# Attention and a routed expert layer on one core: the place of "V times the experts' rows" and of the divisions in the queues, and a second key slot of each head that meets V in float32

## The chip, the cores and the metric

The kernel runs on one core of a Trainium2 chip. The metric is device time in microseconds (us) of that core. Each core has TensorE (PE in the profile; its weight loads are PEld), VectorE (DVE), ScalarE (ACT), GpSimd (POOL) and SyncE (SP), which here only issues DMAs. Each engine works through its own queue in the order of the program and waits at an instruction whose operands or buffers aren't ready.

## The reference

Attention with rotary positions over 4 batches of 8 heads, 576 positions, 64 columns a head; its output, as 2304 tokens of 512 columns, goes through a layer of 8 experts of which each token uses the one with the largest logit.

```python
q_rot, k_rot = (rotate(q), rotate(k))
scores = scale * np.matmul(q_rot, k_rot.transpose(0, 1, 3, 2))
attn = np.exp(scores - np.max(scores, axis=-1, keepdims=True))
attn = attn / (np.sum(attn, axis=-1, keepdims=True) + 1e-09)
x = np.matmul(attn, v)             # then (tokens, heads * 64)
logits = (x / norm(x)) @ (emb / norm(emb)).T / tau
expert_idx = np.argmax(logits, axis=1)
out[mask] = gate_w[mask, None] * (np.maximum(x[mask] @ w1[e], 0.0) @ w2[e])
```

## The kernel before

**Attention.** The 32 heads are 16 pairs (`i`), four to a batch. In a pair the 576 keys of each head are cut into slots of 128; the two last halves of 64 share slot 4, so a pair has 9 slots `s`: 0 to 3 and half of 4 for the first head, 5 to 8 and the other half for the second. For each slot:

- `smm` (tile `st`, lines L208 and L211): TensorE makes the scores, keys in the partitions, 576 queries in the columns.
- `sexp` (tile `p`, L221): ScalarE takes exp into a float32 tile. Its upper 16 bits of each number are read as bfloat16 (`hi`).
- `ssub` (L230): VectorE writes `p - hi` as float16 into the lower half (`lo`). A slot that is `whole` (key slot 0 of each head before) has no `ssub`.
- `maxmm`/`maxmm2` and `maxred` (tile `mx`, L171, L183 and L187): the scores of a later pair, queries in the partitions, and VectorE's maximum over them; `mx` 4 and pairs `s`, `s+5`.
- `pv` (tile `pv`, L246 to L251): probabilities times V for 128 queries, over the five key slots of the head. A slot that isn't whole costs three 16-bit matmuls (`hi` with V's upper part, `hi` with its lower part, `lo` with its upper part); a whole slot costs one float32 matmul, which the trace shows as two.

`st` and `mx` share three PSUM buffers; a new tile takes the buffer whose reader stands earliest in the program, and TensorE waits until that reader is done. `pv` of query slots 0 to 4 lies in PSUM bank 0, of 5 to 8 in bank 1.

V's tile has 73 columns a part: one for the row sum, 64 of V and 8 that are V times the experts' rows, made by `ve`: part 0 are five float32 matmuls into bank 1 (tile `ve`, L112, ten in the trace), then ScalarE copies them out (L116 and L117) and VectorE makes their lower part (L118). `pvend` makes the reciprocals of the row sums on VectorE (L262 and L265), and `pvscale` divides on ScalarE: two instructions (L276 and L277) for each query slot, which are what frees the bank.

**The order** is written out by hand: each step is put at a time `g` in units of one slot (`g0 = 9 * i` is the start of a pair's scores, its `pv` follow `PVL` = 7.5 slots later), all are sorted by it and issued so on every engine. `TIMES` holds these numbers. `spare` finds places for the routing steps that need a PSUM bank, from the list `free` (from, to, bank; in slots of the `pv` period). A batch's squares (`square`) and the write of its rows (`write_x`) follow its last pair.

**Routing and experts.** Ranks and lists of tokens are made on VectorE with a few matmuls (`rank`, `list`); 22 tiles of tokens then go through the experts, their float32 weights being split into two float16 parts by ScalarE (L683) and VectorE (L684).

The slots' places in the order before:

```python
y = g0 + PVL - 9 + cfg.get("vet", 1) + (cfg.get("ve0", 0) if i == 0 else 0)
ev("VE0", y, ve, i, 0)
ev("VE1", y + .9, ve, i, 1)
```

Of the kernel before, what the change touches and what calls it, by code (L numbers as in the profile page):

```python
# [16 lines left out]
B, H, S, D = 4, 8, 576, 64  # L17
# [1 line left out]
SHIFT = 44.375  # L19
VS = 16.0  # L20

NF = 1
GUARD = float(1e-9 * np.exp(0.125 * SHIFT) * VS)


# [7 lines left out]
SY = SX * SW * SW  # L33

ORDER = ((0, 0, 0), (1, 0, 0), (0, 0, 1), (1, 0, 1), (0, 1, 0), (1, 1, 0))
TIMES = {"pe1": 1.06, "pvlead": 7.5, "mend": 11.5, "fin": 3, "w": 0.3, "pbufs": 13, "vat": -1, "med": 0.3, "sst": 1.6, "mct": 0.25, "pvt": 0.3, "pe0": 0.9, "d": 0.6, "rdt": 0.9, "e": 0.5, "c0": 135, "fin2": 2.5, "sq": 0.8, "max0": [[-21, 0.5], [-5, 1], [4.5, 0.9]], "start": [-30, -13, -4, 2.6], "le": -3.5, "vet": 1.2, "mmt": 0.2, "mlead": 14, "klo": 1, "me0": [-13.5, 6.6], "mdir": 3, "ve0": -16, "v0": 3, "pl": [[0, 0, 0, 0], [0, 3, 2, 5]], "setup": [-59.5, -25, -20.9, -19.2, -59.4, -14], "l3": -12, "rk": 14, "ls": 52, "dt": 0.6, "t0": 148.5, "ta": 0.25, "wlead": 10, "cut1": 126, "glead": 20, "s": 0.6, "fin3": -0.45, "r01": [[-30.0, -29.1, -28.2, -27.3, -24.6, -26.4, -25.5, -23.7, -22.8, -21.0], [-25, -24.9, -24.8, -15.5, -14, -20.8, -20.7, -20.6, -15, -13.5]], "bw": 0, "cp": [0, 2, 4, 6], "c0d": 1, "lg1": 0.5, "free": [[2.3, 2.3, 1], [3.5, 3.5, 1], [6.2, 6.2, 0]], "fgap": 1.2}


def attention(tc, ctx0, ctx, ctx2, ins, xs, R, at, bank, cfg):
# [34 lines left out]
    st = {}  # L74
# [31 lines left out]
    def ve(i, k):  # L106

        d = V16[i % NV]
        if k == 0:
            ps = st["ve", i] = bank("ve", 1)  # L110
            for j in range(5):
                nc.tensor.matmul(ps[:, 0:80].rearrange("p (h j e) -> p j h e", h=2, j=5)[:, j], lhsT=st[i]["vt"][:, j], rhs=R.enB[:, i % 4],  # L112
                                 start=True, stop=True)
        else:
            ps = st.pop(("ve", i))[:, 0:80].rearrange("p (s e) -> p s e", e=8)
            nc.scalar.activation(out=d[:, :, 65:73], in_=ps, func=AF.Copy, scale=VS)  # L116
            nc.scalar.activation(out=V32[i % NV][:, :, :, 65:73], in_=ps.rearrange("p (h k) e -> p h k e", h=2)[:, :, 0:NF], func=AF.Copy, scale=VS)  # L117
# [163 lines left out]
    PVL = cfg.get("pvlead", 7)  # L281
# [3 lines left out]
    start = cfg["start"]  # L285
    O = cfg.get("o", {})

    def ev(key, g, f, *a):
        at(g + O.get(key, 0), f, *a)

    for i in range(NPAIR):
        g0 = 9 * i
        r0 = start[i] if i < len(start) else g0 - L - RL
        rdt = cfg.get("rdt", .85)
        if i == 1:
            for nm in "qk":
# [455 lines left out]
class Schedule:  # L752
# [3 lines left out]
    def at(self, g, f, *a):  # L756
        self.T.append((g, len(self.T), f, a))
# [13 lines left out]
def build(tc, ins, out, cfg=None):  # L771
    cfg = {**TIMES, **(cfg or {})}
    nc = tc.nc
    with ExitStack() as ctx:
# [10 lines left out]
        R = Routing(tc, ctx, ins, xs, bank)  # L785
        rp = ctx.enter_context(tc.tile_pool(name="raw", bufs=1))
        raw = [rp.tile([128, 1024], F32, name=f"raw{c}") for c in range(8)]
        sc = Schedule()
        mctx, actx2, actx, actx0 = [ctx.enter_context(ExitStack()) for _ in range(4)]
        if True:  # L790
            PVL = attention(tc, actx0, actx, actx2, ins, xs, R, sc.at, bank, cfg)
# [81 lines left out]
            at = lambda G, *a: sc.at(T0 + DT * G, *a)  # L873
# [114 lines left out]
```

## Time and profile before

| | us |
|---|---|
| median of three runs | 629.57 (628.33 to 630.09) |
| the profiled execution's own time | 627.74 |
| its span, first to last instruction | 626.0 |

The profiled execution has 1.7 us around its span and is 1.8 us under the median. Busy times of the whole span are means over stages with different limits: a start of about 60 us, the 16 pairs, a change-over near 350 to 390 us, and the experts' tiles until the end. The pairs have to be read by themselves.

### The profile page before, as it was taken

Reading aid. Unit: us, or ns where it says so; the run is one execution under the profiler, and the core shown is the slowest. Engines: PE = TensorE matmul, PEld = TensorE weight load, DVE = VectorE, ACT = ScalarE, POOL = GpSimd, SP = SyncE. Lnnn points to the kernel's source line nnn. Section 1 sums busy time; section 2 is a strip of 40 time slices with the busy share of each in tenths; the row PEclk is TensorE's granted clock in tenths of the full one; section 3 lists DMA queues with packets and bytes.
Section 4 is the critical chain, followed back from the end, with each engine's and each line's share of the span. In section 5 each row is a group of like instructions: output and inputs, shape, how many; then the busy total and the mean of one; then the engine's idle time right before and its main releaser. Section 6 shows DMA issues by size and latency. Waiting matters only on the chain. (4 is left out here: it accounts for less than half of the span.)

```text
span 626.0 us, 16246 instructions
## 1 busy us (share of the span) xinstructions
PE 536.7 (86%) x6222; PEld 400.3 (64%) x6222; DVE 514.5 (82%) x750; ACT 394.5 (63%) x848; POOL 256.3 (41%) x162
## 2 busy tenths in 40 slices
PE   1689788877987798778788898999999999999993
PEld 0336657665765575656566786777768677776861
DVE  6987987788778977896777556569999999999991
ACT  2152564567546755544745776258989899898972
POOL 6667764467446754471000333221414233242311
PEclk9999997889878988787878899999999999999997
DMA  8486645465645475513401731137888312441100
GB/s 292 117 235 176 161 134 160 120 165 164 166 118 132 136 217 135 148 31 92 141 24 39 268 116 35 37 102 235 282 309 279 134 35 72 168 176 52 52 20 29
DMA packets 42914, 86.13 MB, mean 138 GB/s; under 512 B 8390, under 2 KB 25670, under 8 KB 42832
## 3 DMA queue, kind: packets, MB, share of 16 engines
q1 hardware_dynamic: 39312, 74.46, 39.9%
q0 software_dynamic: 3520, 10.58, 5.3%
q8 instruction: 51, 0.84, 0.6%
q14 instruction: 31, 0.25, 0.1%
HBM read 115.84 MB, written 10.56 MB: 202 GB/s over the span
## 5 line engine op out<-in xcount | busy, mean ns | idle before, releaser
L684 DVE SCALAR_TENSOR_TENSOR w<-raw,w 128x1024 f16<-128x1024 f32 x148 | 177.1, 1237 | 9.3 <-ACT w L683 9.1
L221 ACT ACTIVATE p<-st 128x576 f32<-128x576 f32 x144 | 94.7, 662 | 122.4 <-PE st L211 122.3
L683 ACT ACTIVATE w<-raw 128x1024 f16<-128x1024 f32 x148 | 148.6, 1056 | 0.2
L187 DVE TENSOR_REDUCE m<-mx 128x1 f32<-128x576 f32 x144 | 105.0, 748 | 36.5 <-PE mx L171 19.2
L230 DVE TENSOR_TENSOR p<-p 128x576 f16<-128x576 f32 x112 | 131.2, 1174 | 1.7 <-ACT p L221 1.7
L720 PEld LDWEIGHTS <-w 128*128 128x128 f16 x2112 | 119.7, 98 | 5.6 <-issue 0.9
L720 PE MATMUL h<-xTm,w 128*128 128x128 f16 x2112 | 122.2, 219 | 0.8 <-DVE xTm L706 0.8
L741 PE MATMUL yp<-w,hT 128*128 128x512 f16 x528 | 120.9, 379 | 0.2 <-POOL w L681 0.2
L746 POOL DMA_INDIRECT out<-y,sidx x22 | 32.9, 1495 | 160.3 <-ACT y L745 160.3
L249 PE MATMUL pv<-V,p 128*128 128x73 f16 (+1 forms) x640 | 89.5, 208 | 0.0
L250 PE MATMUL pv<-V,p 128*128 128x72 f16 (+1 forms) x640 | 89.3, 209 | 0.0
L251 PE MATMUL pv<-V,p 128*128 128x73 f16 (+1 forms) x640 | 89.1, 207 | 0.0
L741 PEld LDWEIGHTS <-hT 128*128 128x128 f16 x528 | 50.7, 98 | 53.3 <-issue 0.7
L208 PE MATMUL st<-QAB,KA 128*128 128x288 f16 (+1 forms) x320 | 70.2, 328 | 10.3 <-DVE m L187 8.4
L249 PEld LDWEIGHTS <-p 128*128 128x128 bf16 (+1 forms) x640 | 76.0, 119 | 0.0
L211 PE MATMUL st<-QAB,KB 65*128 65x288 f16 (+1 forms) x320 | 69.9, 325 | 0.0
L251 PEld LDWEIGHTS <-p 128*128 128x128 f16 (+1 forms) x640 | 69.2, 110 | 0.0
L250 PEld LDWEIGHTS <-p 128*128 128x128 bf16 (+1 forms) x640 | 68.6, 108 | 0.0
L246 PE MATMUL pv<-V,p 128*128 128x73 f32 (+1 forms) x320 | 67.6, 297 | 0.3 <-ACT mr L198 0.2
L246 PEld LDWEIGHTS pv<-V,p 128*128 128x128 f32 (+1 forms) x320 | 52.4, 205 | 18.7 <-issue 15.2
L112 PE MATMUL ve<-enB,vt 128*128 128x16 f32 x160 | 28.8, 320 | 37.3 <-ACT xe L277 37.3
L138 POOL TENSOR_TENSOR qlo<-q,qhi 128x576 f16<-128x576 f32 x14 | 19.2, 1368 | 94.6 <-ACT qhi L133 94.6
(159 smaller groups left out, 760.3 us busy)
## 6 DMA issues: line engine op xcount, KB each, us to landing
raw<-w SPq DMA_DIRECT2D x152, 512.0 KB
q<-qk SPq DMA_DIRECT2D x16, 576.0 KB
k<-qk SPq DMA_DIRECT2D x16, 576.0 KB
vt<-vt SPq DMA_DIRECT2D x16, 320.0 KB
v<-v SPq DMA_DIRECT2D x16, 320.0 KB
QAB<-qhi SPq DMA_DIRECT2D x32, 144.0 KB
KA<-khi SPq DMA_DIRECT2D x64, 72.0 KB
xs<-x SPq DMA_DIRECT2D x8, 512.0 KB
```

Source lines behind the costliest of these rows:

```text
L187: nc.vector.tensor_reduce(out=st[i]["m9"][:, s:s + 1], in_=st.pop(("mx", i, s))[:, :, :288], op=ALU.max, axis=AX.XY)
L208: nc.tensor.matmul(ps[r0:r0 + m, c, :288], lhsT=KA[n][:, col], rhs=QA[n][:, h * S + c * 288:h * S + c * 288 + 288], start=True, stop=False)
L221: nc.scalar.activation(out=p.rearrange("p (c x) -> p c x", c=2), in_=st.pop(("s", i, s))[:, :, :288], func=AF.Exp, scale=0.125)
L230: nc.vector.tensor_tensor(out=lo, in0=p, in1=hi, op=ALU.subtract)
L246: nc.tensor.matmul(o[:, 0:73], lhsT=P[ksl][0][:, qc:qc + m], rhs=V32[i % NV][:, h, kk], start=(kk == 0), stop=False, skip_group_check=True)
L249: nc.tensor.matmul(o[:, 0:73], lhsT=ph, rhs=vv[:, 0:73], start=(kk == 0), stop=False, skip_group_check=True)
L250: nc.tensor.matmul(o[:, 1:73], lhsT=ph, rhs=vv[:, 73:145], start=False, stop=False, skip_group_check=True)
L251: nc.tensor.matmul(o[:, 0:73], lhsT=pl, rhs=vv[:, 0:73], start=False, stop=(kk == 4), skip_group_check=True)
L683: nc.scalar.activation(out=d[:, 0], in_=raw[c], func=AF.Copy, scale=SW)
L684: nc.vector.scalar_tensor_tensor(out=d[:, 1], in0=raw[c], scalar=SW, in1=d[:, 0], op0=ALU.mult, op1=ALU.subtract)
L720: nc.tensor.matmul(ps[:, f], lhsT=wd[:, wi, jj * 512 + f * 128:jj * 512 + f * 128 + 128], rhs=xt[:, xi, 2 * jp + jj], start=(jp == 0 and k ...
L741: nc.tensor.matmul(ps, lhsT=ht[:, hi, 2 * c + ii], rhs=wd[:, wi, ii * 512:(ii + 1) * 512], start=(c == 0 and k == 0), stop=(c == 3 and k = ...
```

## The change

`NF` goes from 1 to 2: key slots 0 and 1 of each head (s = 0, 1, 5, 6) are whole, so two `ssub` of a pair go, each `pv` block has two float32 matmuls and three times three of 16 bits (before one and four times three), and V's float32 tile and the two ScalarE copies that fill it have two slots a head. `vet` goes from 1.2 to 2.9: part 0 of `ve` stands 1.7 slots later, and with it the load of the next pair's `vt`. Its copies come 0.6 slots behind it (0.9 before), and VectorE's lower part is a step of its own, 1.5 behind it. The divisions of a bank begin 0.4 slots after the reciprocals and stand 0.15 apart (at once and 0.2 before). The squares of batches 0 to 2 come 0.45 slots later, their `write_x` 0.25. `free` moves. Of the long line `TIMES` only the two entries that differ are shown.

```diff
-NF = 1
+NF = 2
-TIMES: "vet": 1.2, "free": [[2.3, 2.3, 1], [3.5, 3.5, 1], [6.2, 6.2, 0]]
+TIMES: "vet": 2.9, "free": [[1.9, 1.9, 1], [4.4, 4.4, 1], [6.5, 6.5, 0]]
...
-        else:
+        if k == 1:
             ps = st.pop(("ve", i))[:, 0:80].rearrange("p (s e) -> p s e", e=8)
             nc.scalar.activation(out=d[:, :, 65:73], in_=ps, func=AF.Copy, scale=VS)
...
+            st["ver", i] = ps
+            return
+        if k == 2:
+            ps = st.pop(("ver", i))
             nc.vector.scalar_tensor_tensor(out=d[:, :, 137:145], in0=ps, scalar=VS, in1=d[:, :, 65:73], op0=ALU.mult, op1=ALU.subtract)
...
-        ev("VE1", y + .9, ve, i, 1)
+        ev("VE1", y + .6, ve, i, 1)
+        ev("VE2", y + 1.5, ve, i, 2)
...
-                        at(g0 + PVL + s + cfg.get("pe1", 1.06) + .002 + .2 * j, pvscale, i, s // 5, j)
+                        at(g0 + PVL + s + cfg.get("pe1", 1.06) + .4 + .15 * j, pvscale, i, s // 5, j)
...
-                        sc.at(done + .8 * k if k < 5 else end + .02 + (cfg.get("sq", .6) if b < B - 1 else .05) * (k - 5), R.square, b, k)
+                        sc.at((.45 if b < B - 1 else 0) + done + .8 * k if k < 5 else (.45 if b < B - 1 else 0) + end + .02 + (cfg.get("sq", .6) if b < B - 1 else .05) * (k - 5), R.square, b, k)
-                sc.at(end + (.05 if b == B - 1 else .7), R.write_x, b)
+                sc.at(end + (.05 if b == B - 1 else .95), R.write_x, b)
```

What stands in the queues around `ve` of pair 5. In a name, the first two numbers of `st`, `p` and `mx` are pair and slot, `mx_6_2` being query slot 2 of pair 6; `pv_20` is the first half of pair 4, `pv_18` the second half of pair 3, and the last number only counts tiles.

TensorE before: `ve` follows the maxima of slots 2 and 7, and behind it comes `pv` of pair 4, query slot 1, with one float32 matmul ahead of the 16-bit ones.

```order
L183 LDWEIGHTS qhi_6_1251
L183 MATMUL mx_6_2_1790<-khi_6_1425,qhi_6_1251 128x288
L183 LDWEIGHTS qhi_6_1251
L183 MATMUL mx_6_7_1791<-khi_6_1425,qhi_6_1251 128x288
L112 MATMUL ve_21_1806<-enB_73,vt_5_1483 128x2x8 x5
L246 MATMUL pv_20_1763<-V32_0_143,p_4_0_1511 128x73
L249 LDWEIGHTS p_4_1_1537
L249 MATMUL pv_20_1763<-V16_0_141,p_4_1_1537 128x73
L250 LDWEIGHTS p_4_1_1537
L250 MATMUL pv_20_1763<-V16_0_141,p_4_1_1537 128x72
L251 LDWEIGHTS p_4_1_1537
L251 MATMUL pv_20_1763<-V16_0_141,p_4_1_1537 128x73
```

TensorE now: it follows the maxima of slots 3 and 8, and behind it comes query slot 3 with two float32 matmuls.

```order
L187 LDWEIGHTS qhi_6_1195
L187 MATMUL mx_6_3_1761<-khi_6_1358,qhi_6_1195 128x288
L187 LDWEIGHTS qhi_6_1195
L187 MATMUL mx_6_8_1762<-khi_6_1358,qhi_6_1195 128x288
L112 MATMUL ve_21_1768<-enB_73,vt_5_1467 128x2x8 x5
L250 MATMUL pv_20_1669<-V32_0_143,p_4_0_1431 128x73
L250 MATMUL pv_20_1669<-V32_0_143,p_4_1_1452 128x73
L253 LDWEIGHTS p_4_2_1488
L253 MATMUL pv_20_1669<-V16_0_141,p_4_2_1488 128x73
L254 LDWEIGHTS p_4_2_1488
L254 MATMUL pv_20_1669<-V16_0_141,p_4_2_1488 128x72
L255 LDWEIGHTS p_4_2_1488
```

So `ve` has moved past two `pv` blocks (slots 1 and 2), the scores `st_5_0` and `st_5_1`, and the maxima of slots 3 and 8.

ScalarE before, from the first division of bank 1 on: three slots are divided, then V's copies, the exp of `st_4_8`, the last slot.

```order
L276 ACTIVATE x_0_656<-pv_18_1624,pvr_3_1_1755 128x64
L277 ACTIVATE xe_0_657<-pv_18_1624,pvr_3_1_1755 128x8
L276 ACTIVATE x_0_656<-pv_18_1624,pvr_3_1_1755 128x64
L277 ACTIVATE xe_0_657<-pv_18_1624,pvr_3_1_1755 128x8
L276 ACTIVATE x_0_656<-pv_18_1624,pvr_3_1_1755 128x64
L277 ACTIVATE xe_0_657<-pv_18_1624,pvr_3_1_1755 128x8
L99 ACTIVATE V16_1_142<-v_5_1474 128x10x64
L100 ACTIVATE V32_1_144<-v_5_1474 128x2x64
L221 ACTIVATE p_4_8_1786<-st_4_8_1779 128x576
L276 ACTIVATE x_0_656<-pv_18_1624,pvr_3_1_1755 128x64
L277 ACTIVATE xe_0_657<-pv_18_1624,pvr_3_1_1755 128x8
```

ScalarE now:

```order
L280 ACTIVATE x_0_641<-pv_18_1536,pvr_3_1_1666 128x64
L281 ACTIVATE xe_0_642<-pv_18_1536,pvr_3_1_1666 128x8
L99 ACTIVATE V16_1_142<-v_5_1404 128x10x64
L100 ACTIVATE V32_1_144<-v_5_1404 128x4x64
L225 ACTIVATE p_4_8_1690<-st_4_8_1683 128x576
L280 ACTIVATE x_0_641<-pv_18_1536,pvr_3_1_1666 128x64
L281 ACTIVATE xe_0_642<-pv_18_1536,pvr_3_1_1666 128x8
L280 ACTIVATE x_0_641<-pv_18_1536,pvr_3_1_1666 128x64
L281 ACTIVATE xe_0_642<-pv_18_1536,pvr_3_1_1666 128x8
L280 ACTIVATE x_0_641<-pv_18_1536,pvr_3_1_1666 128x64
L281 ACTIVATE xe_0_642<-pv_18_1536,pvr_3_1_1666 128x8
```

One slot is divided ahead of the exp instead of three, three behind it; the number of instructions up to the last division is the same.

VectorE before, from the reciprocal of bank 1 to the lower part of `ve`:

```order
L265 RECIPROCAL pvr_3_1_1755<-pvr_3_1_1755 128x4
L230 TENSOR_TENSOR p_4_6_1713<-p_4_6_1713 128x576
L187 TENSOR_REDUCE m9_6_1653<-mx_6_2_1790 128x1
L230 TENSOR_TENSOR p_4_7_1746<-p_4_7_1746 128x576
L104 SCALAR_TENSOR_TENSOR V16_1_142<-v_5_1474,V16_1_142 128x10x64
L138 TENSOR_TENSOR klo_7_1833<-k_7_1191,khi_7_1748 128x576
L187 TENSOR_REDUCE m9_6_1653<-mx_6_7_1791 128x1
L230 TENSOR_TENSOR p_4_8_1786<-p_4_8_1786 128x576
L118 SCALAR_TENSOR_TENSOR V16_1_142<-ve_21_1806,V16_1_142 128x10x8
```

VectorE now:

```order
L269 RECIPROCAL pvr_3_1_1666<-pvr_3_1_1666 128x4
L191 TENSOR_REDUCE m9_6_1566<-mx_6_2_1694 128x1
L234 TENSOR_TENSOR p_4_7_1657<-p_4_7_1657 128x576
L104 SCALAR_TENSOR_TENSOR V16_1_142<-v_5_1404,V16_1_142 128x10x64
L142 TENSOR_TENSOR klo_7_1729<-k_7_1133,khi_7_1659 128x576
L191 TENSOR_REDUCE m9_6_1566<-mx_6_7_1695 128x1
L234 TENSOR_TENSOR p_4_8_1690<-p_4_8_1690 128x576
L191 TENSOR_REDUCE m9_6_1566<-mx_6_3_1761 128x1
L191 TENSOR_REDUCE m9_6_1566<-mx_6_8_1762 128x1
L122 SCALAR_TENSOR_TENSOR V16_1_142<-ve_21_1768,V16_1_142 128x10x8
```

The subtraction of slot 6 is gone (that of slot 1 too, further down), and the lower part of `ve` stands behind the maxima of slots 3 and 8.

## Rows read from the trace of the kernel before

**Rows 1.** The page: the span.

```profile
span 626.0 us, 16246 instructions
```

**Rows 2.** Busy time by stage. Columns: the stretch in us, its length, busy us (instructions) of PE, PEld, DVE, ACT and POOL, mean granted clock of TensorE (1.00 is the full one), DMA share, GB/s.

```profile
25.00:63.00 38.00, 34.87 (x196) 19.70 (x196) 30.44 (x35) 14.06 (x28) 25.26 (x15) 1.00 0.64 172
75.00:258.50 183.50, 150.72 (x1900) 116.32 (x1900) 150.53 (x213) 110.24 (x341) 103.06 (x63) 0.88 0.54 148
258.50:348.00 89.50, 72.33 (x864) 55.54 (x864) 68.58 (x160) 47.25 (x154) 17.99 (x12) 0.83 0.28 75
426.00:600.00 174.00, 174.00 (x1966) 129.48 (x1964) 173.76 (x175) 154.11 (x192) 53.50 (x31) 1.00 0.46 155
```

**Rows 3.** The one instruction that each pair has once on ScalarE (the negated maxima, L198), in two stretches: number, duration in ns (least/median/most), first and last start in us.

```profile
L198 ACT ACTIVATE mr<-mt,shiftt x10: 343/358/360, 69.7 to 253.4; 9x128 f16<-9x128 f32 x10
...
L198 ACT ACTIVATE mr<-mt,shiftt x5: 343/343/359, 253.4 to 343.9; 9x128 f16<-9x128 f32 x5
```

**Rows 4.** Who waited for whom: engine, tile and line of the waiting instruction, what it waited for, us in total, times, the longest. The first four are of 75 to 258.5 us, the next two of 258.5 to 348 us, the last of the whole span.

```profile
PE ve L112 <- ACT xe L277: 27.3, 10, 2.8
DVE V L118 <- ACT V L117: 12.7, 9, 3.0
PE st L208 <- DVE m L187: 6.6, 9, 0.8
PE mx L183 <- DVE m L187: 1.7, 9, 0.2
...
PE ve L112 <- ACT xe L277: 10.3, 4, 2.7
PE rank L488 <- ACT xe L277: 2.7, 1, 2.7
...
PE rank L485 <- ACT xe L277: 2.0, 1, 2.0
```

**Rows 5.** TensorE in order of time, around `ve` of pair 4: start in us, duration in us (with the way through the array, so that neighbours overlap), line, operation, out<-in, shape, number; in brackets the idle time before and what ended it.

```profile
111.08 0.41 PE L208 MATMUL st<-QAB,KA 128*128 128x288 f16 x2
111.57 0.34 PE L246 MATMUL pv<-V,p 128*128 128x73 f32 x2
111.75 0.20 PE L249 MATMUL pv<-V,p 128*128 128x73 f16 x1
...
111.85 0.20 PE L249 MATMUL pv<-V,p 128*128 128x73 f16 x1
...
112.16 0.41 PE L208 MATMUL st<-QAB,KA 128*128 128x288 f16 x2
112.74 0.42 PE L183 MATMUL mx<-khi,qhi 64*128 64x288 f16 x4
115.93 1.29 PE L112 MATMUL ve<-enB,vt 128*128 128x16 f32 x10 [2.77 <-ACT xe L277]
117.07 0.42 PE L246 MATMUL pv<-V,p 128*128 128x73 f32 x2
```

**Rows 6.** ScalarE in the same stretch, with the same columns.

```profile
112.94 0.32 ACT L276 ACTIVATE x<-pv,pvr 128x64 f32<-128x64 f32 x1
...
113.99 0.80 ACT L99 ACTIVATE V<-v 128x640 f16<-128x640 f32 x1
...
114.83 0.69 ACT L221 ACTIVATE p<-st 128x576 f32<-128x576 f32 x1
...
115.55 0.32 ACT L277 ACTIVATE xe<-pv,pvr 128x8 f32<-128x8 f32 x1
```

**Rows 7.** VectorE in the same stretch.

```profile
112.77 1.76 DVE L230 TENSOR_TENSOR p<-p 128x576 f16<-128x576 f32 x1
114.43 0.73 DVE L187 TENSOR_REDUCE m<-mx 128x1 f32<-128x576 f32 x1
115.08 1.33 DVE L230 TENSOR_TENSOR p<-p 128x576 f16<-128x576 f32 x1
...
117.71 0.74 DVE L187 TENSOR_REDUCE m<-mx 128x1 f32<-128x576 f32 x1
118.38 0.79 DVE L230 TENSOR_TENSOR p<-p 128x576 f16<-128x576 f32 x1
...
122.76 0.82 DVE L230 TENSOR_TENSOR p<-p 128x576 f16<-128x576 f32 x1
```

**Rows 8.** Three stretches on end: behind `ve` of pair 4, from there to that of pair 5, and behind it, with the columns of the second group.

```profile
117.70:121.00 3.30, 3.30 (x30) 2.38 (x29) 1.73 (x4) 0.86 (x3) 0.00 (x0) 0.50 0.82 221
121.10:134.60 13.50, 11.08 (x165) 8.13 (x161) 11.88 (x17) 10.28 (x32) 10.48 (x7) 1.00 0.43 122
134.80:141.40 6.60, 5.57 (x43) 5.27 (x44) 4.46 (x7) 2.23 (x9) 0.90 (x1) 0.50 0.84 241
```

**Rows 9.** TensorE in order of time at two other places: `ve` of pair 1, and `ve` of pair 3 with the matmuls behind it.

```profile
50.31 2.31 PE L112 MATMUL ve<-enB,vt 128*128 128x16 f32 x10
...
94.91 2.31 PE L112 MATMUL ve<-enB,vt 128*128 128x16 f32 x10 [2.77 <-ACT xe L277]
97.06 0.68 PE L246 MATMUL pv<-V,p 128*128 128x73 f32 x2
97.54 0.27 PE L249 MATMUL pv<-V,p 128*128 128x73 f16 x1
...
97.73 0.26 PE L249 MATMUL pv<-V,p 128*128 128x73 f16 x1
```

More of the change, by code (lines that the diff above doesn't have):

```diff
@@ L35 @@
 ORDER = ((0, 0, 0), (1, 0, 0), (0, 0, 1), (1, 0, 1), (0, 1, 0), (1, 1, 0))
-TIMES = {"pe1": 1.06, "pvlead": 7.5, "mend": 11.5, "fin": 3, "w": 0.3, "pbufs": 13, "vat": -1, "med": 0.3, "sst": 1.6, "mct": 0.25, "pvt": 0.3, "pe0": 0.9, "d": 0.6, "rdt": 0.9, "e": 0.5, "c0": 135, "fin2": 2.5, "sq": 0.8, "max0": [[-21, 0.5], [-5, 1], [4.5, 0.9]], "start": [-30, -13, -4, 2.6], "le": -3.5, "vet": 1.2, "mmt": 0.2, "mlead": 14, "klo": 1, "me0": [-13.5, 6.6], "mdir": 3, "ve0": -16, "v0": 3, "pl": [[0, 0, 0, 0], [0, 3, 2, 5]], "setup": [-59.5, -25, -20.9, -19.2, -59.4, -14], "l3": -12, "rk": 14, "ls": 52, "dt": 0.6, "t0": 148.5, "ta": 0.25, "wlead": 10, "cut1": 126, "glead": 20, "s": 0.6, "fin3": -0.45, "r01": [[-30.0, -29.1, -28.2, -27.3, -24.6, -26.4, -25.5, -23.7, -22.8, -21.0], [-25, -24.9, -24.8, -15.5, -14, -20.8, -20.7, -20.6, -15, -13.5]], "bw": 0, "cp": [0, 2, 4, 6], "c0d": 1, "lg1": 0.5, "free": [[2.3, 2.3, 1], [3.5, 3.5, 1], [6.2, 6.2, 0]], "fgap": 1.2}
+TIMES = {"pe1": 1.06, "pvlead": 7.5, "mend": 11.5, "fin": 3, "w": 0.3, "pbufs": 13, "vat": -1, "med": 0.3, "sst": 1.6, "mct": 0.25, "pvt": 0.3, "pe0": 0.9, "d": 0.6, "rdt": 0.9, "e": 0.5, "c0": 135, "fin2": 2.5, "sq": 0.8, "max0": [[-21, 0.5], [-5, 1], [4.5, 0.9]], "start": [-30, -13, -4, 2.6], "le": -3.5, "vet": 2.9, "mmt": 0.2, "mlead": 14, "klo": 1, "me0": [-13.5, 6.6], "mdir": 3, "ve0": -16, "v0": 3, "pl": [[0, 0, 0, 0], [0, 3, 2, 5]], "setup": [-59.5, -25, -20.9, -19.2, -59.4, -14], "l3": -12, "rk": 14, "ls": 52, "dt": 0.6, "t0": 148.5, "ta": 0.25, "wlead": 10, "cut1": 126, "glead": 20, "s": 0.6, "fin3": -0.45, "r01": [[-30.0, -29.1, -28.2, -27.3, -24.6, -26.4, -25.5, -23.7, -22.8, -21.0], [-25, -24.9, -24.8, -15.5, -14, -20.8, -20.7, -20.6, -15, -13.5]], "bw": 0, "cp": [0, 2, 4, 6], "c0d": 1, "lg1": 0.5, "free": [[1.9, 1.9, 1], [4.4, 4.4, 1], [6.5, 6.5, 0]], "fgap": 1.2}
 def attention(tc, ctx0, ctx, ctx2, ins, xs, R, at, bank, cfg):
@@ L835, in build @@
                     if b < 2:
-                        sc.at((done if k < 5 else end + .02) + cfg.get("sq0", 2.5) * (k % 5) + cfg.get("sq1", 12) * (k > 4), R.square, b, k)
+                        sc.at((done if k < 5 else end + .02) + .45 + cfg.get("sq0", 2.5) * (k % 5) + cfg.get("sq1", 12) * (k > 4), R.square, b, k)
                     else:
-                        sc.at(done + .8 * k if k < 5 else end + .02 + (cfg.get("sq", .6) if b < B - 1 else .05) * (k - 5), R.square, b, k)
-                sc.at(end + (.05 if b == B - 1 else .7), R.write_x, b)
+                        sc.at((.45 if b < B - 1 else 0) + done + .8 * k if k < 5 else (.45 if b < B - 1 else 0) + end + .02 + (cfg.get("sq", .6) if b < B - 1 else .05) * (k - 5), R.square, b, k)
+                sc.at(end + (.05 if b == B - 1 else .95), R.write_x, b)
                 if b < 2:
```

## The prediction

> **What bounds the kernel now.** The page gives the span, 626.0 us [rows 1], and means over unlike stages. The busy times by stage say where to look. In the experts' tiles (426 to 600 us) TensorE and VectorE are busy without a gap at the full clock, and the change touches nothing there. In the pairs (75 to 258.5 us) VectorE has 150.53 of 183.50 us, ScalarE 110.24, GpSimd 103.06, and TensorE, for all its 150.72, runs at a mean granted clock of 0.88 [rows 2]. No engine is full, so the pairs are held by waits.
>
> One instruction of each pair gives the period: (253.4 - 69.7) / 9 = 20.41 us, and (343.9 - 253.4) / 4 = 22.6 us for the next four, which carry routing steps too [rows 3]. The waits name the largest loss: TensorE stood still 27.3 us in ten times at `ve`, for ScalarE's divisions (`xe`), and 10.3 us in four more later; its other waits, for VectorE, come to 8.3 us in nine pairs, 0.92 us each [rows 4]. TensorE's own order shows how: the maxima are issued at 112.74, `ve` starts at 115.93 after 2.77 us of idling [rows 5], right where ScalarE's last division of bank 1, started at 115.55, ends at 115.87 [rows 6]. All that stands behind `ve` waits with it, the next scores too, whose exps ScalarE then lacks and whose maxima VectorE lacks.
>
> The bubble costs twice. From 117.7 to 121.0, and behind the next pair's `ve` from 134.8 to 141.4, the granted clock is 0.50, that is 1.2 GHz, with the bubble ahead of it each time [rows 8]. A mean of 0.88 means that 24% of the time is at half clock, 0.24 x 20.41 = 4.9 us a pair, of which half, 2.45 us, is lost. TensorE's own work at full clock is then 20.41 - 2.77 - 0.92 - 2.45 = 14.27 us a pair.
>
> **The change, part by part.** *`ve` later.* I walk the new order from the scores of slot 7 (111.08, called 0), with 0.49 us for scores (111.08 to 111.57), 0.59 for a `pv` block (111.57 to 112.16) and 1.14 for `ve` (115.93 to 117.07) [rows 5], and about 0.4 for two maxima (0.42 with the way through the array). A `pv` block gets 0.125 longer (below). Slot 7, `pv` 0, slot 8, two maxima, `pv` 1, scores 0, `pv` 2, scores 1 come to 4 x 0.49 + 3 x 0.71 + 0.4 = 4.5 us, where the maxima of slots 3 and 8 and then `ve` stand. The last division ends where it did, since as many instructions stand ahead of it: 115.87 - 111.08 = 4.8, plus about 0.1 for V's larger copy. That is about when `ve` can come at the earliest, so the 2.77 us go. The exp of slot 8, which the scores of slot 1 need for their buffer, has two divisions less ahead of it; from 114.83 and 0.69 us long it now starts some 0.7 earlier (three take from 112.94 to 113.99, 0.35 each [rows 6]) and ends near 3.8, when the walk has the scores of slot 1 at 4.1: no wait.
>
> What comes up instead is the buffer for the maxima of slot 3: it is that of slot 7, whose reduction is late on VectorE. Before, from the reduction of slot 2 (114.43) to the end of that of slot 7 (117.71 + 0.74) it took 4.0 us [rows 7], with a subtraction, V's lower part and a subtraction for K between, all of which stay. Slot 2's maxima are there at 2.2, so slot 7 is reduced at 6.2, and TensorE, there at 4.6, waits 1.6 us. Towards the pair's end a reduction is late again (the 0.92 us of before); three long subtractions are still ahead of it, and I take 1.0. So 2.6 us of waits stand where 3.69 were.
>
> *Two subtractions fewer.* Those of slots 6 and 1 took 1.76 us (112.77) and 0.82 (122.76) [rows 7], 2.6 us of VectorE a pair. VectorE isn't full, so by itself this is worth nothing; it pays in that the reductions come early enough for the walk above. It has cover: VectorE's 16.7 us a pair (150.53 / 9) fall to 14.1. If the subtractions that stay take longer, each is paid in the 1.6 us wait.
>
> *More float32.* A slot that becomes whole swaps three 16-bit matmuls for two float32 ones per block. Three take 0.10 us at full clock (111.75 to 111.85) [rows 5] and 0.19 at half (97.54 to 97.73) [rows 9]. For a float32 one behind another the trace has `ve`, ten with weights of the same shape: 1.14 us at full clock, 0.228 for two [rows 5]; at half clock 97.06 - 94.91 = 2.15, 0.43 for two [rows 9]. So +0.125 us a block at full clock, +0.24 at half. Eight blocks and a ninth of half-sized pieces (0.05) make +1.05 us a pair, +2.0 at half. The lower bound is nothing, if loads hide behind the stream. The Trainium skill's page "FP8 and Floating Point Precision", section "TensorE Precision Notes", has true float32 as four passes through the array; by that alone the estimate would be 4 x 73 columns against 3 x 73, a third more stream, 0.03 us a block, some 0.3 us a pair and a total some 10 us lower. The rows differ: `ve` has 16 columns and is no quicker, so it isn't columns that I count.
>
> *The rest.* `ve`'s lower part on VectorE falls behind two reductions, ending near 9; `pv` of bank 1, which needs it, is some 2 us further: slack. The 12.7 us that VectorE waited at it [rows 4] go with the bubble. V's float32 copies on ScalarE grow by about 0.1 us, in ScalarE's spare 40%. Squares, `write_x` and the load of `vt` move by less than a slot or two and are needed a pair later or more. `rank` waited 2.7 and 2.0 us for divisions [rows 4] and now has a `pv` block and scores more ahead of it: I take 1.5 us off for both.
>
> *Sum.* A pair: 14.27 + 1.05 + 2.6 = 17.92, or 2.49 less, if the clock stays up: the longest idle time is then 1.6 us. Nine pairs: -22.4. The four with routing have the same bubble (10.3 / 4 = 2.6) and a clock of 0.83, but more VectorE steps; I take 2.3 each: -9.2. The last pair has the fourteenth of the waits, behind the last of these periods; I count it like the four: -2.3. `rank` -1.5. Pairs 0 and 1 have no bubble, and `ve` of pair 1 took 2.31 us like the slow one of pair 3 [rows 9], so TensorE, busy 34.87 of 38 us there [rows 2], pays for float32: +1.1 (a block +0.24 at half clock, four and a half of them). Together -34.3: 627.74 - 34.3 = 593.4 for the profiled execution; the median of before lies 1.8 above its own, so **595 us**.
>
> **The rivals.**
> *The clock still falls once a pair.* For: the new wait of 1.6 us stands close ahead of `ve`, whose small matmuls are a thin load. Against: the waits for VectorE of up to 0.8 us that every pair has today [rows 4] bring none, for between two pairs' falls the clock is 1.00 for 13.5 us [rows 8]. A stretch of 3.3 us at half clock [rows 8] costs 1.7 a pair, 13 x 1.7 = 22: **about 617**.
> *The new waits mostly don't come*, because VectorE, with 14.1 us of work, runs ahead: waits stay at today's 0.92, 1.7 us a pair less, 13 x 1.7 = 22: **about 573**. Against: 4.0 us of VectorE work stand between the two reductions whatever comes earlier.
> *No gain.* The clock stays down for as long as now, 4.9 us a pair: 14.27 + 1.05 + 2.45 + 2.6 = 20.37, the period of today; what is left is the little around it: **about 625**.
> *Slower: float32 and a cold clock.* Should the clock fall at both waits of a pair, about 10 us of it would be at half, and float32 costs double there: 15.32 + 5.1 + 1 of waits (VectorE has more time) = 21.4, 1.0 more than now, 13 us in all less the small gains: **about 640**. It decides from some 6 us at half clock a pair; today's 4.9 would only balance.
>
> **How the numbers follow.** Within 0.3% (1.9 us) of the median a measurement of this kernel doesn't tell a change from none. Chances: the forecast 0.50 (586 to 604 us), a fall a pair 0.22, fewer waits 0.10, no gain 0.07, slower 0.09, in between 0.02. Faster 0.83, same 0.07, slower 0.10. The likeliest case's own range is 586 to 604; the range for 8 in 10 reaches into the fall a pair and halfway to the case with fewer waits, 578 to 618.
>
> **What would show it.** The wait of `ve` for `xe` gone from the waits. L198's period 17.5 to 18.4 us. A wait of TensorE's maxima (L187 in the new file) for VectorE of 1 to 2 us a pair. Mean granted clock above 0.95 from pair 2 on. Subtractions down from 112 to 80. The experts' stretch as full as now, only earlier. Wrong it would be if the half clock is seen again behind `ve`, if the float32 blocks cost more than 0.73 us, or if VectorE turns out to be late by more than 1.6 us.

## The result and the profile after

Before 629.28 us (628.33 to 630.09), after **609.63 us** (607.31 to 619.5), four runs each; the ratio is 0.9676 with a 95% interval of 0.9635 to 0.9717. The profiled execution of after took 608.31 us with a span of 606.5 us, 19.5 less than the 626.0 of [rows 1]; forecast was a span shorter by 34.3. One of the four executions of after (619.5) took over 1.5% longer than the fastest; such executions, here and in some runs below, count in medians and ranges but not in the ratios. The change made the kernel faster, by some 57% of the expected amount. 609.63 us lies in the range for 8 in 10 (578 to 618), but outside the likeliest case's own 586 to 604 and nearer to "a fall a pair" (about 617) than to 595.

After, the page's span, and a stretch of the experts' tiles with the columns of [rows 2].

```profile
span 606.5 us, 15880 instructions
...
406.00:580.00 174.00, 174.00 (x1974) 129.88 (x1972) 173.71 (x176) 153.76 (x190) 54.50 (x31) 1.00 0.46 158
```

The period's instruction is now L202 (it was L198), over nine pairs and the next four, as in [rows 3]:

```profile
L202 ACT ACTIVATE mr<-mt,shiftt x10: 342/358/359, 71.0 to 239.3; 9x128 f16<-9x128 f32 x10
...
L202 ACT ACTIVATE mr<-mt,shiftt x5: 342/343/358, 239.3 to 317.3; 9x128 f16<-9x128 f32 x5
```

Nine periods take 168.3 us (18.70 each; 183.7 before), the next four 78.0 (19.5; 90.5 before). The experts' stretch is as full as it was: 174.00 of 174.00 us on TensorE at the full clock. From before to after the gains and losses are: start 69.7 to 71.0, 1.3 us lost; nine pairs, 15.4 won; four more, 12.5 won; and from the last pair's L202 (343.9, now 317.3) to the end 282.1 before, 289.2 after, 7.1 lost. That is the whole -19.5.

Who waited for whom, of the whole span of after (columns as in [rows 4]):

```profile
PE mx L187 <- DVE m L191: 10.9, 16, 1.1
PE mx L187 <- ACT p L225: 7.3, 15, 0.9
```

`ve` and its 37.6 us of [rows 4] (27.3 and 10.3) are gone from the list. The maxima wait instead, for VectorE's reductions or ScalarE's exps, whichever had their buffer last (scores and maxima take turns in one pool); and `list`, which had no such wait, waits 4.4 us (below). The nine pairs one by one, with the columns of [rows 2]:

```profile
71.00:90.90 19.90, 18.73 (x204) 14.60 (x204) 13.43 (x22) 11.57 (x35) 11.10 (x8) 0.83 0.54 156
90.90:109.10 18.20, 17.35 (x203) 13.62 (x202) 12.79 (x22) 11.38 (x34) 9.60 (x7) 0.91 0.55 151
109.10:126.50 17.40, 15.86 (x203) 12.50 (x202) 14.53 (x22) 12.19 (x39) 11.03 (x8) 1.00 0.57 158
126.50:146.40 19.90, 17.41 (x204) 13.49 (x203) 14.83 (x22) 12.58 (x40) 12.41 (x9) 0.91 0.68 198
146.40:166.40 20.00, 18.68 (x203) 14.62 (x202) 13.34 (x22) 12.18 (x38) 10.99 (x8) 0.83 0.51 138
166.40:184.70 18.30, 17.50 (x204) 13.79 (x204) 14.10 (x26) 12.34 (x39) 10.92 (x8) 0.91 0.55 150
184.70:202.00 17.30, 15.82 (x202) 12.46 (x202) 14.47 (x22) 12.15 (x38) 10.96 (x8) 1.00 0.57 159
202.00:222.20 20.20, 17.46 (x204) 13.61 (x204) 15.13 (x22) 12.62 (x41) 12.46 (x9) 0.92 0.70 195
222.20:239.30 17.10, 15.55 (x202) 12.37 (x202) 13.51 (x22) 12.15 (x38) 9.60 (x7) 1.00 0.57 161
```

Three pairs keep the full clock and take 17.1 to 17.4 us; six have a stretch at half clock, 1.2 GHz, and take 18.2 to 20.2. In the first kind the walk of the prediction can be laid beside TensorE's order of time (pair at 109.60, the scores of slot 7):

```profile
109.60 0.41 PE L212 MATMUL st<-QAB,KA 128*128 128x288 f16 x2
...
110.09 0.56 PE L250 MATMUL pv<-V,p 128*128 128x73 f32 x4
...
110.80 0.41 PE L212 MATMUL st<-QAB,KA 128*128 128x288 f16 x2
...
115.09 0.28 PE L187 MATMUL mx<-khi,qhi 64*128 64x288 f16 x1 [0.58 <-ACT p L225]
115.63 0.40 PE L187 MATMUL mx<-khi,qhi 64*128 64x288 f16 x3 [0.26 <-ACT p L225]
115.96 0.28 PE L112 MATMUL ve<-enB,vt 128*128 128x16 f32 x1
...
125.86 0.42 PE L187 MATMUL mx<-khi,qhi 64*128 64x288 f16 x4 [0.69 <-DVE m L191]
```

A `pv` block takes 110.80 - 110.09 = 0.71 us. `ve` starts 6.36 us behind the scores of slot 7 with no wait of its own. Ahead of it the maxima wait 0.58 + 0.26 = 0.84 us, and at the pair's end 0.69.

The loss of 7.1 us lies in the change-over. From the last pair's L202 to the first `h`, the experts' first matmul with weights, it took 24.6 us before (343.9 to 368.5) and takes 31.5 now (317.3 to 348.8):

```profile
L720 PE MATMUL h<-xTm,w x2112: 216/219/220, 368.5 to 605.8; 128*128 128x128 f16 x192
```

```profile
L725 PE MATMUL h<-xTm,w x2112: 216/219/220, 348.8 to 586.4; 128*128 128x128 f16 x192
```

It shows on ScalarE, VectorE and TensorE behind the last pair's `ve` (321.66):

```profile
323.97 1.06 ACT L684 ACTIVATE ws<-raw 128x1024 f32<-128x1024 f32 x1 [2.37 <-issue]
...
326.56 1.05 ACT L688 ACTIVATE w<-raw 128x1024 f16<-128x1024 f32 x1
...
328.03 0.27 ACT L116 ACTIVATE V<-ve 128x80 f16<-128x80 f32 x1
```

```profile
327.63 1.82 DVE L689 SCALAR_TENSOR_TENSOR w<-raw,w 128x1024 f16<-128x1024 f32 x1 [6.22 <-ACT w L688]
...
329.51 0.25 DVE L122 SCALAR_TENSOR_TENSOR V<-ve,V 128x80 f16<-128x80 f32 x1
```

```profile
321.66 1.29 PE L112 MATMUL ve<-enB,vt 128*128 128x16 f32 x10
329.81 0.94 PE L542 MATMUL list<-B,Aoh 128*128 128x4 f16 x30 [4.38 <-DVE V L122]
333.99 1.13 PE L250 MATMUL pv<-V,p 128*128 128x73 f32 x4 [2.26 <-DVE lst L547]
```

The copy of the last pair's `ve` (L116) stands behind the first conversions of the experts' weights (L684 to L688). It runs 6.4 us after `ve` started. VectorE's lower part (L122) needs that copy, and it stands behind VectorE's own half of the conversions too (L689), which ends at 329.45. `list` waits for L122, and TensorE then works at half clock until 341.6:

```profile
328.00:341.60 13.60, 9.53 (x91) 7.64 (x90) 6.19 (x13) 7.61 (x20) 6.93 (x6) 0.50 0.59 197
```

### The profile page after: what moved, and what is told of

It reads as the page before. It is cut to its first block, busy times and chain, and to the rows that moved or that the text cites. A ratio compares the mean times of both kernels' runs of the same rounds, so it can differ in the third digit from the quotient of the medians.

```text
span 606.5 us, 15880 instructions
## 1 busy us (share of the span) xinstructions
PE 543.8 (90%) x6062; PEld 409.3 (67%) x6062; DVE 476.6 (79%) x718; ACT 394.5 (65%) x848; POOL 248.6 (41%) x162
## 5 line engine op out<-in xcount | busy, mean ns | idle before, releaser
L689 DVE SCALAR_TENSOR_TENSOR w<-raw,w 128x1024 f16<-128x1024 f32 x148 | 177.7, 1240 | 16.1 <-ACT w L688 15.8
L688 ACT ACTIVATE w<-raw 128x1024 f16<-128x1024 f32 x148 | 148.3, 1055 | 0.0
L250 PE MATMUL pv<-V,p 128*128 128x73 f32 (+1 forms) x640 | 103.7, 290 | 4.7 <-DVE lst L547 2.3
L250 PEld LDWEIGHTS pv<-V,p 128*128 128x128 f32 (+1 forms) x640 | 86.4, 198 | 24.3 <-issue 16.9
L234 DVE TENSOR_TENSOR p<-p 128x576 f16<-128x576 f32 x80 | 91.5, 1147 | 3.3 <-ACT p L225 3.2
L253 PE MATMUL pv<-V,p 128*128 128x73 f16 (+1 forms) x480 | 71.0, 208 | 0.0
L254 PE MATMUL pv<-V,p 128*128 128x72 f16 (+1 forms) x480 | 70.8, 209 | 0.0
L255 PE MATMUL pv<-V,p 128*128 128x73 f16 (+1 forms) x480 | 70.2, 206 | 0.0
L215 PE MATMUL st<-QAB,KB 65*128 65x288 f16 (+1 forms) x320 | 66.8, 315 | 0.9 <-DMA QAB<-mr 0.9
L212 PE MATMUL st<-QAB,KA 128*128 128x288 f16 (+1 forms) x320 | 66.3, 315 | 0.3 <-ACT p L225 0.2
L253 PEld LDWEIGHTS <-p 128*128 128x128 bf16 (+1 forms) x480 | 58.9, 123 | 0.0
L280 ACT ACTIVATE x<-pv,pvr 128x64 f32<-128x64 f32 x135 | 44.9, 333 | 14.4 <-DVE pvr L269 14.4
L255 PEld LDWEIGHTS <-p 128*128 128x128 f16 (+1 forms) x480 | 52.7, 111 | 0.0
L254 PEld LDWEIGHTS <-p 128*128 128x128 bf16 (+1 forms) x480 | 52.2, 109 | 0.0
```

The source lines that it names most:

```text
L215: nc.tensor.matmul(ps[r0:r0 + m, c, :288], lhsT=KB[n][0:65, col], rhs=QB[n][0:65, h * S + c * 288:h * S + c * 288 + 288], start=False, sto ...
L234: nc.vector.tensor_tensor(out=lo, in0=p, in1=hi, op=ALU.subtract)
L250: nc.tensor.matmul(o[:, 0:73], lhsT=P[ksl][0][:, qc:qc + m], rhs=V32[i % NV][:, h, kk], start=(kk == 0), stop=False, skip_group_check=True)
L253: nc.tensor.matmul(o[:, 0:73], lhsT=ph, rhs=vv[:, 0:73], start=(kk == 0), stop=False, skip_group_check=True)
L254: nc.tensor.matmul(o[:, 1:73], lhsT=ph, rhs=vv[:, 73:145], start=False, stop=False, skip_group_check=True)
L255: nc.tensor.matmul(o[:, 0:73], lhsT=pl, rhs=vv[:, 0:73], start=False, stop=(kk == 4), skip_group_check=True)
```

## The experiments

The kernel before ran beside each group: 631.59 us (628.52 to 635.06) for the first four runs, 629.5 (626.34 to 634.5) for the next four, 628.82 (626.76 to 630.25) for the last two. Where the text compares with after, it is 609.63 us and the ratio 0.9676. "Nine pairs" are always the stretch between the first and the tenth L202 (L198 in the old file) from about 70 us on. Of `TIMES` only the entries that differ are shown. The moves of the squares, of `write_x` and of `free` were not undone by themselves.

**Undo one part at a time.** One float32 slot, all moves kept:

```diff
-NF = 2
+NF = 1
```

> The changed kernel with all its moves, but with one float32 slot per head as before (NF = 1; 112 subtractions instead of 80). Theory 'both are needed': VectorE, with 2.6 us more a pair, reduces slot 7 later, TensorE waits some 3 us before the maxima of slot 3 where it now waits about 0.7, and the clock falls in nearly every pair: 620 to 630. Rival 'the distance alone does it, and float32 only costs its 1.05 us a pair': 593 to 605.

Measured: 618.21 us (615.98 to 620.17), ratio 0.9788 (0.9726 to 0.985). TensorE's waits in the nine pairs, then the nine pairs:

```profile
PE mx L187 <- DVE m L191: 14.4, 15, 1.6
PE st L212 <- DVE m L191: 10.2, 8, 1.3
PE mx L187 <- ACT p L225: 1.7, 3, 0.6
```

```profile
71.40:244.40 173.00, 146.54 (x1900) 112.58 (x1899) 143.42 (x211) 109.10 (x339) 100.73 (x63) 0.91 0.57 156
```

Between both theories (620 to 630 and 593 to 605): the moves alone win 13.4 us, but 26.3 us of waits stand in nine pairs, 24.6 of them for VectorE, against 13.7 in those of after (8.9 and 4.8). The mean clock, 0.91, is hardly under after's 0.92, so that part of "both are needed" is wrong.

The other half, the second float32 slot in the old places:

```diff
 in the kernel before:
-NF = 1
+NF = 2
```

> The kernel before with the second float32 slot alone (NF = 2), `ve` and the divisions where they were. Theory: TensorE's wait at `ve` for ScalarE's divisions stays (about 2.5 us, once a pair) and the clock falls with it, while float32 costs 1 to 1.5 us a pair: 630 to 645. Rival (what helps is VectorE's relief, wherever `ve` stands): under 620.

Measured: 638.99 us (635.29 to 642.29), ratio 1.0101 (1.0036 to 1.0165).

```profile
PE ve L112 <- ACT xe L277: 37.6, 14, 3.1
```

```profile
L198 ACT ACTIVATE mr<-mt,shiftt x10: 342/358/360, 69.1 to 253.6; 9x128 f16<-9x128 f32 x10
...
253.60:356.10 102.50, 86.96 (x839) 68.51 (x838) 61.40 (x148) 49.13 (x158) 19.71 (x14) 0.73 0.25 66
```

The total and the wait are as the theory has them, the way is not: the nine pairs take 184.5 us against 183.7 before, hardly a price at all (their mean clock is 0.92, against 0.88 in [rows 2]), and the loss is in the four routing pairs, 102.5 us against 90.5, at a clock of 0.73 (0.83 in [rows 2]). The profiled execution was the slowest of the four, 642.29 us. **The same edit costs 7 us where `ve` waits for ScalarE, and wins 7 to 9 us (618.21 against 609.63, ratios 0.9788 and 0.9676) where `ve` has been moved.** That fits VectorE's relief being worth something only once VectorE is what TensorE waits for. It is not shown to be all: the 7 us lie in the routing pairs, at a lower clock, and not in all pairs alike, as a float32 price would.

`ve` back in its old place, everything else as changed:

```diff
-"vet": 2.9
+"vet": 1.2
```

> The changed kernel with vet 1.2 for 2.9: `ve` stands where it stood before, the divisions' spacing and the second float32 slot stay. Theory (the place of `ve` behind the divisions is what removed the 2.8 us bubble): the wait of `ve` for `xe` comes back at 2.3 to 3.5 us in most pairs and the time is 633 to 645, like the 639.0 of the kernel before with the float32 slot alone. Rival (the spacing of the divisions brings them early enough by itself): 608 to 620.

Measured: 653.08 us (648.47 to 661.46), ratio 1.0376 (1.031 to 1.0442), more than either theory gave.

```profile
PE ve L112 <- ACT xe L281: 36.6, 14, 3.5
```

The old wait is back. `ve`'s place is what removes it. Why this is another 14 us over the run with the float32 slot alone stays open. Part of it lies in the executions: the two profiled ones (648.47 and 642.29 us) are 6.2 apart, with 4.3 in the nine pairs (188.8 and 184.5) and 5.7 in the change-over, less 4.5 in the routing pairs. The edit also leaves the squares and `free` at places that were chosen for the later `ve`.

The divisions' spacing back, everything else as changed:

```diff
-  at(g0+PVL+s+cfg.get("pe1",1.06) + .4 + .15*j, pvscale, ...)
+  at(g0+PVL+s+cfg.get("pe1",1.06) + .002 + .2*j, pvscale, ...)
```

> The changed kernel with the divisions' spacing alone as before (.002 + .2 a division instead of .4 + .15). Theory from the prediction (the last division of bank 1 ends where it did, since as many instructions stand ahead of it, and `ve` is now late enough for it): no wait at `ve` comes back, within 3 us of the changed kernel's 609.6. Rival (the spacing is part of the gain: the exps of slots 8 and 4 behind fewer divisions keep the maxima supplied): 612 to 622, with longer waits of the scores or the maxima for ScalarE's `p`.

Measured: 605.69 us (604.27 to 611.17), ratio 0.9643 (0.9583 to 0.9702), which overlaps that of after; the median is 3.9 us below it, 0.9 more than the 3 that were expected. `ve` shows no wait; the divisions' spacing bought nothing that these runs can tell.

**The change-over to the experts.** The first weight conversions two slots later:

```diff
-"c0": 135
+"c0": 137.1
```

> The changed kernel with one number of the table moved, c0 from 135 to 137.1: the first conversions of the experts' weights come two slots later in ScalarE's queue, so that the last pair's copies of `ve` stand ahead of the first of them. Theory (early conversions hold the last pair's copies back; from there follow the 4.4 us that `list` waits, the 2.3 us of the `pv` behind it and some 13.7 us at half clock): `list` waits under 1 us, and 9 to 13 us less than the changed kernel, about 598. Rival (the end of the attention is held by something else, the weights' arrival or VectorE's reductions): within 2 us of the changed kernel's 609.6.

Measured: 607.68 us (604.2 to 612.95), ratio 0.9652 (0.958 to 0.9724): no difference that can be told from after, as the rival had it (within 2 us). `list` waits no more, but this came up (TensorE, then VectorE in order of time):

```profile
PE pv L250 <- DVE lst L547: 3.8, 1, 3.8
...
326.68 1.82 DVE L689 SCALAR_TENSOR_TENSOR w<-raw,w 128x1024 f16<-128x1024 f32 x1 [4.93 <-ACT w L688]
...
328.56 0.15 DVE L547 COPY lst<-list 128x4 f32<-128x4 f32 x1
```

The cause named was right for `list` and too narrow for the time: the conversions stand in VectorE's queue too. VectorE idles 4.93 us at L689 for ScalarE's conversion of the same weights, with the copy of `list` behind it. From the last pair's L202 to the first `h` it takes 29.2 us here, against 24.6 before and 31.5 after:

```profile
L202 ACT ACTIVATE mr<-mt,shiftt x16: 341/357/359, 27.0 to 315.4; 9x128 f16<-9x128 f32 x16
L725 PE MATMUL h<-xTm,w x2112: 216/219/219, 344.6 to 582.3; 128*128 128x128 f16 x192
```

**What fills the wait ahead of `ve`.** `ve` in front of the maxima of slots 3 and 8:

```diff
-"vet": 2.9
+"vet": 2.65
```

> The changed kernel with vet 2.65 for 2.9: on TensorE `ve` stands ahead of the maxima of slots 3 and 8 instead of behind them. Theory (the wait before those maxima is for VectorE's reduction of slot 7, and `ve`, 1.14 us that needs no VectorE, fills it): that wait goes from 8.0 us in twelve to under 3, `ve` meets its divisions just done, the clock falls in fewer pairs, 0.8 to 2 us a pair less: 587 to 599. Rival (the last division ends too late, so `ve` waits as before the change, or the wait moves to the next maxima): 606 to 615.

Measured: 600.22 us (598.0 to 607.08), ratio 0.9542 (0.9463 to 0.9622), at the upper edge of the interval expected (598.91 in the median without the slowest execution). Waits and time of the nine pairs:

```profile
PE mx L187 <- DVE m L191: 6.3, 11, 1.0
...
68.40:225.00 156.60, 147.84 (x1811) 115.93 (x1810) 129.37 (x194) 109.51 (x339) 101.12 (x65) 0.96 0.64 178
```

In the nine pairs the maxima's waits go from 13.7 us to 6.3 (those for ScalarE are gone, those for VectorE fell less than expected; the scores have new ones of 2.4 us in all), the clock from 0.92 to 0.96, the period from 18.70 to 17.40. Of the 11.7 us won there 5.0 are waits. The rest is about what the clock gives: by the mean clocks some 26.9 us were at half clock (0.16 of 168.3) and 12.5 are (0.08 of 156.6), and half of the difference is 7.2, an estimate.

Both numbers moved, the conversions this time behind `list`'s copy as well:

```diff
-"vet": 2.9
+"vet": 2.65
-"c0": 135
+"c0": 138.6
```

> The changed kernel with two numbers of its table moved: vet 2.65 (`ve` ahead of the maxima of slots 3 and 8 on TensorE, as in the run that moved `ve` alone, 600.2 us) and c0 138.6 (the first weight conversion of ScalarE behind the last pair's copies of `ve`, and that of VectorE behind the copy of `list`). Theory (the change-over from the last attention pairs to the experts lost 7 us to conversions that stand ahead of these two small copies; moving only the first copy, as in the run with c0 137.1, left `pv` waiting 3.8 us for `lst` and the clock at half for 10 us): from the last pair's L202 to the first `h` matmul it takes 24 to 27 us, as the 24.6 of the kernel before, where the run with `ve` moved alone took 32.3; the total is 5 to 8 us under 600.2, about 593. Rival (the experts' weights are then converted too late and the first `h` waits for them instead): 597 to 602, with `h` waiting for VectorE's or ScalarE's conversions.

Measured: **593.06 us** (589.28 to 598.51, six runs), ratio 0.9418 (0.9367 to 0.9468). The total came as expected, the change-over did not: 304.0 to 333.7 are 29.7 us, not 24 to 27. So the total is right in part by luck: of the 7.2 us against 600.22 the change-over gave 2.6 (32.3 us there, 29.7 here), and 3.0 came in the nine pairs, whose order is the same in both runs (156.6 and 153.6). `list` and `lst` are out of the waits, and the gather of the experts' rows is in:

```profile
PE xps L704 <- DMA xg<-xs,gidx: 4.5, 1, 4.5
```

```profile
313.08 0.16 DVE L546 TENSOR_SCALAR gidx<-list 128x4 int32<-128x4 f32 x1 [0.67 <-PE list L542]
```

```profile
322.28 2.14 POOL L686 TENSOR_TENSOR w<-ws,w 128x1024 f16<-128x1024 f32 x1 [3.74 <-ACT w L685]
324.59 1.97 POOL L698 DMA_INDIRECT xg<-xs,gidx  x1 [0.18 <-issue]
```

Its indices are ready at 313.24, and GpSimd issues it at 324.59, behind the second of its own weight conversions, which the later c0 holds back. So each wait taken out of the change-over uncovered the next queue with conversions in it; ScalarE's, VectorE's and GpSimd's were met in turn, and 5.1 of the 7 us stay. The nine pairs took 153.6 us here, 17.07 each, at a clock of 0.98.

**Is VectorE the cause?** A third float32 slot on after alone:

```diff
-NF = 2
+NF = 3
```

> The changed kernel with three float32 slots per head and nothing else altered (vet 2.9, c0 135). Theory (TensorE's wait before the maxima of slots 3 and 8 is for VectorE's late reduction of slot 7, and that wait brings the clock down): with some 2.4 us less work on VectorE a pair the waits of the maxima for VectorE fall from 10.9 us to under 5, the clock falls in none to two of the nine pairs instead of five or six, the nine periods come to 16.5 to 17.3 us, and the total is 594 to 603 with the loss at the change-over still in it. Rival (the float32 price on TensorE, 1 us a pair, is what counts): 615 to 622.

Measured: 604.35 us (599.67 to 616.68), ratio 0.9596 (0.9522 to 0.967), at the upper edge of the interval expected (601.77 in the median without the slowest execution).

```profile
PE mx L187 <- DVE m L191: 3.6, 7, 0.8
...
69.70:231.30 161.60, 157.32 (x1721) 126.00 (x1720) 106.91 (x176) 110.28 (x339) 94.22 (x64) 0.95 0.61 171
...
77.66:81.07 3.41, 3.41 (x30) 2.76 (x30) 0.26 (x1) 1.28 (x4) 0.00 (x0) 0.50 0.85 243
```

The waits fall as the theory says. The clock does not follow it: 0.95, four of the nine pairs with a half-clock stretch, and a period of 17.96 us where 16.5 to 17.3 was expected. Less waiting alone doesn't keep the clock up. The first fall, at 77.66, follows a `ve` (76.19) ahead of which the trace lists no wait, and two pairs with a wait of 0.57 us ahead of `ve` (111.94 and 128.99) had none. With `ve` ahead of the maxima, and more waiting (8.7 us), the clock stood a little higher (0.96 and 0.98 in the two runs with that order).

Three, then four slots on the version with both numbers moved:

```diff
-"vet": 2.9
+"vet": 2.65
-"c0": 135
+"c0": 138.6
-NF = 2
+NF = 3
```

> The version with both numbers moved (vet 2.65, c0 138.6) and three float32 slots per head (NF = 3: 48 subtractions instead of 80; eight more float32 pairs of matmuls a pair of heads for 24 16-bit ones). Theory A (TensorE is by now what holds a pair, with waits of about 0.7 us left, so each slot costs its float32 price of about 1 us a pair and VectorE's relief brings nothing): 10 to 16 us more than with two slots, 603 to 610. Theory B (what is left of the waits and the falls of the clock comes from VectorE's late reductions): within 4 us of the version with two slots, or under it.

Measured: **587.48 us** (585.17 to 603.07), ratio 0.9321 (0.9264 to 0.9379): theory B, the third slot still wins 5.6 us; the two intervals just touch. This is the fastest version that ran. Against it:

```diff
-NF = 3
+NF = 4
```

> The version with both numbers moved (vet 2.65, c0 138.6) and four float32 slots per head (NF = 4; 16 subtractions are left). With three slots TensorE was busy 16.5 of the 16.5 us of a pair in the profile. Theory A (TensorE is now full and each further slot costs its float32 price, 8 blocks x 0.12 us, about 1 us a pair): 10 to 16 us more than with three slots, 597 to 603. Theory B (VectorE, freed of 2.4 us more, still pays): 580 to 588.

Measured: 591.51 us (589.66 to 593.48), ratio 0.9411 (0.9375 to 0.9448). The nine pairs:

```profile
70.20:226.00 155.80, 155.80 (x1632) 128.85 (x1631) 92.81 (x158) 111.89 (x340) 89.85 (x64) 1.00 0.62 176
```

Neither theory's number: 4 us more than with three slots, not 10 to 16. TensorE is busy 155.80 of 155.80 us at the full clock, so in the nine pairs it is full, as theory A says, and VectorE has 92.81 us, so its relief has nothing left to pay there. The float32 work is the bound: 17.31 us a pair. Theory A had the same price in the routing pairs too, and there it didn't come: the four took 74.2 us at a clock of 0.98, and 79.0 at 0.89 with three slots (in its profiled execution of 597.56 us).

## Why the prediction was right in part, step by step

- *The 2.77 us at `ve` go.* Right. The walk had the last division end at 4.9 us and `ve` start at 6.2 plus two maxima, 6.6. In the pair shown that division (L281, at 114.18 for 0.31 us) ends at 114.49 - 109.60 = 4.89, and `ve` starts at 6.36.
- *A float32 block +0.125 us.* Right: 0.71 forecast, 0.71 measured. The Trainium skill's page "FP8 and Floating Point Precision", section "TensorE Precision Notes", counts four passes for float32; by that a block would have grown by an estimated 0.03 us. The trace gives 0.12, from 0.59 [rows 5].
- *New waits of 1.6 and 1.0 us.* Right in place, too large: 0.84 and 0.69 in the pair shown. The first ends there with ScalarE's exps; the walk had named the reduction of slot 7 on VectorE alone, which in this pair starts only at 115.61. Of the nine pairs four wait ahead of `ve` for the exps, three for that reduction and two for both.
- *Own work 14.27 + 1.05 = 15.32.* Half a microsecond small: 15.86 and 15.82 in the pairs at full clock. With the waits it makes 17.4, where 17.92 was walked: the work that was too small gives back half of the waits that were too large.
- *"If the clock stays up".* **This step failed.** The argument was that the longest idle time would be 1.6 us and that waits up to 0.8 bring no fall. Single waits came out at 1.11 us at most, and six pairs of nine still had a stretch at half clock: mean 0.92 instead of above 0.95, period 18.70 instead of 17.92. By the prediction's own sign, the half clock seen again behind `ve`, the step is wrong. The rival "the clock still falls once a pair" came true in two pairs of three, and its price was near: 26.9 us at half clock cost some 13.5, an estimate, 1.5 a pair where it had 1.7. The measured time is in the range for 8 in 10 because that range reaches into this rival. The rival had also named where the wait stands: close ahead of `ve`. Moving `ve` in front of it brought the clock to 0.96, and with it and less waiting 9 us; that the place of the wait makes the fall is not shown.
- *Four routing pairs and `rank`, -10.7.* Right: -12.5. *Start, +1.1.* Right: +1.3.
- *The last pair, -2.3, "like the four".* **Wrong by 9.4 us:** 7.1 were lost. The step followed `ve` on TensorE and the copies it feeds, but not what stands ahead of these copies in the last pair: conversions of the experts' weights on ScalarE, the first of them behind 2.37 us of idling whose end the profile doesn't explain, and on VectorE. In the kernel before, the first of them stood ahead of `ve`'s copies too, but `list`, from 354.14 us on, waited 0.56 us. Moving the conversions showed the cause for `list`, and was no full cure.

The forecast -34.3 misses by 14.8: 7.0 in the nine pairs (9 x 0.78), 9.4 of the change-over and 0.2 of the start, less 1.8 in the routing pairs. The 7.0 are what is left of larger errors: the clock costs some 13.5 us and the own work 4.5 (9 x 0.5) that weren't in the sum, and the waits are 13.7 us where 23.4 (9 x 2.6) were. That gives 8.3, near to 7.0. So the nine pairs are nearer to the forecast than their parts, which is luck.

Open is what makes the clock fall in one pair and not in the next. The three pairs that kept it waited ahead of `ve` as long as those that didn't, 0.79 to 0.91 us against 0.52 to 1.63:

```profile
228.49 0.42 PE L187 MATMUL mx<-khi,qhi 64*128 64x288 f16 x4 [0.91 <-DVE m L191]
```

Nor does the order of the instructions decide it. The run that moved only the conversions has the same order in these pairs; its fifth pair kept the full clock and took 17.2 us, where that of after took 20.0 at 0.83:

```profile
145.10:162.30 17.20, 15.65 (x204) 12.47 (x203) 13.62 (x22) 12.19 (x38) 9.69 (x7) 1.00 0.57 156
```

## What to carry to other kernels

A stall that is removed leaves its neighbours in every in-order queue where they were: look at what stands ahead of each small consumer in the first and last rounds, where other work (here the conversions of weights) shares the queue. The same edit can cost before a reordering and pay after it, so try the relief of an engine again once the others wait for it. When a stretch depends on the granted clock, forecast both levels with near-even chances, and count the falls in several traces: here the same instructions ran at either level.

## What the runs showed of the hardware

Idle time much shorter than the 2.77 us of [rows 5] can come ahead of a fall of the granted clock: TensorE idled for 0.52 us ahead of the maxima at 172.37 us of after, ran them and `ve`, and from 174.4 us the level was 0.50, that is 1.2 GHz. It needn't bring one: 0.84 us stood ahead of `ve` in the pair at 109.60, which ran at 1.00.

```profile
172.37 0.80 PE L187 MATMUL mx<-khi,qhi 64*128 64x288 f16 x4 [0.52 <-ACT p L225]
...
174.40:177.80 3.40, 3.40 (x32) 2.76 (x32) 1.57 (x5) 1.34 (x4) 2.56 (x2) 0.50 0.77 211
```

With four float32 slots and no such wait all nine pairs ran at 1.00: there more work on TensorE (17.31 us a pair of its own, against 15.8) took less time than the period of after, 18.70.
